# A re-searched instruction order for a fused clustered-attention and gelu kernel, with the last stores on two queues

One core of a Trainium2 chip. The metric is the device time of one execution in microseconds (us), as the median of several executions.

## The reference

Attention over 4 batches x 8 heads (32 "heads" below, numbered 0 to 31), 768 positions, 64 wide, in which a query sees only the keys of its own cluster; then a feed-forward layer without biases.

```python
q_assign = argmax(einsum('bhsd,hcd->bhsc', q_n, c_n), -1)   # 16 clusters; q_n, k_n, c_n normalised
k_assign = argmax(einsum('bhsd,hcd->bhsc', k_n, c_n), -1)
mask   = q_assign[:, :, :, None] == k_assign[:, :, None, :]
scores = where(mask, matmul(q, k^T) / sqrt(D), -1e9)
x      = softmax(scores) @ v          # to 3072 tokens x 512
h      = x @ w_in                     # 512 -> 2048
out    = gelu_exact(h) @ w_out        # 2048 -> 512, float32
```

## The kernel before

Every operation (some matmuls, an exp, a copy, a transfer) is an object with a name, an engine, what it depends on and which buffers it takes. A string, TABLE, lists the names in the order in which they are emitted; `@DVE` behind a name puts that operation on another engine. Nothing is decided at run time: each engine executes its operations in the order of the table, and where an operand isn't there yet, it waits.

```python
TABLE = (
    "cent loadq0 loadq1 zero3 loadk1 dm loadk0 hiq0 zero2 ident ssq ones hik0 exptab root "
    "eps loq0 warm256 warm256 ... warm256 trq0 rnorm lok0 hiq1 loadk2 cn chi warm256 warm256 trk0 "
    # ... cut: about 2000 names ...
    "fc2_3_P7_2_1 u32_3 c222_3@DVE stc2223 fc2_3_P3_2_0 fc2_3_P3_2_1 fc2_3_P4_2_0 "
    "fc2_3_P4_2_1 c122_3 stc1223 c212_3 stc2123 "
)
...
    def run(self, table):
        ...                                        # cut: bookkeeping
        for word in table:
            name, _, eng = word.partition("@")
            if name.startswith("warm"):
                self.filler(int(name[4:]))         # a matmul whose result nobody reads
                continue
            op = by_name[name]
            assert op not in done and done.issuperset(op.deps), name
            ...                                    # cut: takes buffers from their pools
            op.emit(*([eng or op.eng] if op.alt else []))
...
    POOLS = {"raw": 4, "st": 3, "T": 6, ..., "sc": 2, "m": 1, ...}   # buffers of each kind
```

`hi` and `lo` write q and k as a sum of two fp16 numbers into a block `st`; the block is transposed into `kqT`, by TensorE for heads 0 to 9 and by a DMA for heads 10 to 31; then `asn`, the assignment, multiplies it with the centroids.

```python
        if i in PE_TR:                             # heads 0 to 9
            ...                                    # trk / trq on TensorE, evk / evq copy them out
        else:
            def dtr():
                nc.sync.dma_start_transpose(
                    out=new_T().rearrange("p a n d -> p (a n) d"),
                    in_=T["st", i].rearrange("p a n d -> p (a n d)"))
            e = add("SP", 1.4, due - 10, dtr, [sp["k"], sp["q"]], take=[s_T], dma=2.2,
                    name=f"dtr{i}")
            ...
        a1 = add("PE", ad, due + 3, lambda: asn("k"),
                 [ready["k"], c11] + ([ready["q"]] if i > 1 else []), take=[s_m],
                 name=f"asnk{i}")
        a2 = add("PE", ad, due + 3.2, lambda: asn("q"), [ready["q"], a1], name=f"asnq{i}")
```

Names used below: `dtr26` is the DMA transpose of head 26, `asnk26` and `asnq26` its assignment matmuls, `sc` scores (L783 in the kernel before), `av` probabilities times v, `fc1` / `fc2` the two products of the feed-forward layer, `fold`, `amax` and `ge` the steps from the assignment to a one-hot mask, `putk` / `putq` the writing of mask rows into `kqT`, `st...` the stores of results. The middle of each table, which is cut here, is only more of the same.

The softmax here doesn't subtract the row's maximum and nothing guards it: scores larger than these inputs give would overflow.

## Time and profile before

| kernel before | |
|---|---|
| device time, median of 3 (range) | 291.56 us (291.4 to 292.01) |
| span of the core in the profiled run | 289.8 us |
| busy: PE / ACT / DVE / POOL | 98% / 81% / 70% / 37% |
| work of all matmuls, counted by starts | 274.9 us |
| PE idle or stalled inside the span | about 4.6 us of real stalls |

How to read it: the engine names are PE (TensorE), ACT (ScalarE), DVE (VectorE), POOL (GpSimd), SP (SyncE, which issues DMAs). A line of a timeline has the start, the length, the engine, the line of the source, the operation with result<-operands, the size, a count, and in brackets the idle time before it with what ended that. Line numbers of the changed kernels are up to 3 lower than those of the kernel before, since the table is shorter. "By starts" below means: start of a matmul, less the start of the one before, less what the one before needs at full rate (0.109 us for 256 columns, and so on, as the prediction derives). The bracket in a timeline counts from a modelled end and is a little smaller.

### The profile page before, as it was taken

Reading aid. Unit: us, or ns where it says so; the run is one execution under the profiler, and the core shown is the slowest. Engines: PE = TensorE matmul, PEld = TensorE weight load, DVE = VectorE, ACT = ScalarE, POOL = GpSimd, SP = SyncE. Lnnn points to the kernel's source line nnn. Section 1 sums busy time; section 2 is a strip of 40 time slices with the busy share of each in tenths; the row PEclk is TensorE's granted clock in tenths of the full one; section 3 lists DMA queues with packets and bytes.
Section 4 is the critical chain, followed back from the end, with each engine's and each line's share of the span. In section 5 each row is a group of like instructions: output and inputs, shape, how many; then the busy total and the mean of one; then the engine's idle time right before and its main releaser. Section 6 shows DMA issues by size and latency. Waiting matters only on the chain.

```text
span 289.8 us, 8355 instructions
## 1 busy us (share of the span) xinstructions
PE 284.4 (98%) x3398; PEld 213.0 (73%) x3398; DVE 204.2 (70%) x494; ACT 235.1 (81%) x333; POOL 108.0 (37%) x148
## 2 busy tenths in 40 slices
PE   8999999999999999999999999999999999999995
PEld 6887766677677777765677878766687788756884
DVE  4989788397998778643489875725778833787863
ACT  4899988699799999977799988957699988599510
POOL 5898834609120631117202031605622271328000
PEclk9999999999999999999999999999999999999999
DMA  7999998899666799976479899753134213200023
GB/s 249 249 268 248 256 214 230 207 174 177 160 175 139 146 227 187 188 192 168 127 156 177 156 222 187 191 128 75 27 30 118 56 50 97 77 2 0 20 74 127
DMA packets 78038, 43.11 MB, mean 149 GB/s; under 512 B 55472, under 2 KB 78000, under 8 KB 78000
## 3 DMA queue, kind: packets, MB, share of 16 engines
q1 hardware_dynamic: 73488, 38.16, 57.7%
q0 software_dynamic: 4224, 4.19, 8.9%
q8 instruction: 26, 0.43, 0.6%
q10 hardware_dynamic: 288, 0.23, 0.3%
q14 instruction: 12, 0.10, 0.1%
HBM read 27.30 MB, written 6.29 MB: 116 GB/s over the span
## 4 chain that ended last, share of the span: by engine, by line
PE 96%; DVE 2%; ACT 1%; issue 0%; DVEq 0%
PE op L1233 25%; PE hp L918 22%; PE sc_ps L783 21%; PE x_ps L815 12%; PE fx_ps L1054 6%; PE asn_ps L615 2%; PE warm_ps L372 2%; PE tr_ps L573 2%; DVE kqT L714 1%; DVE kqT L723 1%; PE asn_ps L613 1%; PE asn_ps L612 1%; PE oh_ps L691 1%; ACT p_sb L792 1%; PE fin_ps L886 0%
## 5 line engine op out<-in xcount | busy, mean ns | idle before, releaser
L792 ACT ACTIVATE p_sb<-sc_ps 128x768 f16<-128x768 f32 x192 | 146.0, 810 | 9.7 <-PE sc_ps L783 6.8
L783 PE MATMUL sc_ps<-kqT 80*128 80x384 f16 x384 | 93.5, 325 | 0.6 <-DVE kqT L714 0.3
L918 PE MATMUL hp<-xt,w_in_sb 128*128 128x384 f16 x384 | 65.6, 326 | 0.0
L815 PEld LDWEIGHTS <-p_sb 128*128 128x128 f16 x1152 | 47.2, 97 | 10.4 <-DVE x_tok L842 0.6
L1233 PEld LDWEIGHTS <-g 128*128 128x128 f16 x480 | 45.3, 97 | 12.6 <-DVE g L948 0.2
L931 ACT ACTIVATE g<-hp 128x768 f16<-128x768 f32 x48 | 38.9, 810 | 19.0 <-PE hp L918 18.5
L918 PEld LDWEIGHTS <-w_in_sb 128*128 128x128 f16 x384 | 36.4, 98 | 22.9 <-issue 0.2
L815 PE MATMUL x_ps<-vaug,p_sb 128*128 128x65 f16 x1152 | 51.6, 193 | 0.0
L1233 PE MATMUL op<-w_out_sb,g 128*128 128x256 f16 x288 | 40.9, 272 | 0.0
L783 PEld LDWEIGHTS <-kqT 80*128 80x128 f16 x384 | 31.6, 98 | 4.7 <-DVE kqT L714 0.5
L1233 PE MATMUL op<-w_st,g 128*128 128x256 f16 x192 | 27.3, 272 | 0.0
L518 POOL TENSOR_TENSOR st<-k_raw,st 128x384 f16<-128x384 f32 x18 | 17.0, 943 | 24.9 <-DVE st L382 18.4
L518 POOL TENSOR_TENSOR st<-q_raw,st 128x384 f16<-128x384 f32 x21 | 19.8, 947 | 13.4 <-ACT st L380 8.6
L382 POOL CAST st<-q_raw 128x384 f16<-128x384 f32 x16 | 8.4, 531 | 40.9 <-DMA q_raw<-in_q_dram 24.9
L631 DVE TENSOR_REDUCE asb<-asn_ps 128x192 f32<-128x384 f32 x24 | 13.2, 551 | 14.8 <-PE asn_ps L615 14.6
L382 POOL CAST st<-k_raw 128x384 f16<-128x384 f32 x16 | 8.6, 537 | 35.4 <-DMA kqT<-st 16.3
L1233 PEld LDWEIGHTS <-S 128*128 128x128 f16 x192 | 18.0, 97 | 5.0
L842 DVE TENSOR_TENSOR x_tok<-x_ps,rec 128x384 f16<-128x384 f32 (+1 forms) x40 | 19.0, 476 | 1.1
L835 DVE RECIPROCAL rec<-x_ps 128x6 f32<-128x6 f32 (+1 forms) x40 | 7.4, 186 | 11.7 <-PE x_ps L815 10.7
L615 PEld LDWEIGHTS <-kqT 128*128 128x128 f16 x288 | 12.0, 96 | 3.4
L1233 PE MATMUL op<-w_st,S 128*128 128x256 f16 x96 | 13.9, 272 | 0.0
L1233 PE MATMUL op<-w_out_sb,S 128*128 128x256 f16 x96 | 13.8, 272 | 0.0
(125 smaller groups left out, 405.6 us busy)
## 6 DMA issues: line engine op xcount, KB each, us to landing
q_raw<-in_q_dram SPq DMA_DIRECT2D x32, 192.0 KB, 3.5
v_raw<-in_v_dram SPq DMA_DIRECT2D x32, 192.0 KB, 3.5
out_dram<-c SPq DMA_DIRECT2D x48, 128.0 KB, 2.0
k_raw<-in_k_dram SPq DMA_DIRECT2D x31, 192.0 KB, 3.4
w_in_sb<-in_moe_w_in_dram POOLq DMA_DIRECT2D x4, 512.0 KB, 10.4
w_out_sb<-in_moe_w_out_dram POOLq DMA_DIRECT2D x4, 512.0 KB, 8.6
kqT<-st SPq DMA_TRANSPOSE x22, 4.3
k_raw<-in_k_dram ACTq DMA_DIRECT2D x1, 192.0 KB, 3.2
```

Of the source, the lines that this page charges most:

```text
L382: engine[eng].tensor_copy(o, i)
L518: engine[eng].tensor_sub(t[:, :, D:2 * D], T[w + "raw", i], t[:, :, 0:D])
L615: nc.tensor.matmul(o, t[:, js], c_cat[:, h].rearrange("p a c -> p (a c)"), start=True, stop=True)
L631: nc.vector.tensor_reduce(out=T["asb", i], in_=T["asn", i].rearrange("p n w (a c) -> p n w c a", a=2), axis=AX.X, op=ALU.add)
L783: nc.tensor.matmul(s_ps[:, e, 0:QB], T["kT", i][0:D + C, c * 128:(c + 1) * 128], T["qT", i][0:D + C, t * QB:(t + 1) * QB], start=True, sto ...
L792: nc.scalar.activation(T["p", i, t][:, 2 * cp:2 * cp + 2, :], T["sc", i, t, cp][:, :, 0:QB], ACT_FN.Exp, bias=0.0, scale=float(scale))
L815: nc.tensor.matmul(o, T["p", i, t][:, ch, jj * 128:(jj + 1) * 128], vaugs[turn("va", i)][:, ch, 0:D + 1], start=(ch == 0), stop=(ch == N - 1))
L842: nc.vector.tensor_tensor(T["xtok", b][:, h // 2, j0:j0 + nn, h % 2 * D:(h % 2 + 1) * D], T["x", key][:, :, 0:D], T["rec", key].to_broadca ...
L918: nc.tensor.matmul(T["hp", hb, fp][:, e, 0:QB], w_in_sb[:, m, f * 128:(f + 1) * 128], T["xt", b][:, m, t * QB:(t + 1) * QB], start=(m == 0 ...
L931: nc.scalar.activation(T["g", hb][:, :, fp, :], T["hp", hb, fp][:, :, 0:QB], ACT_FN.Gelu, bias=0.0, scale=1.0)
L1054: nc.tensor.matmul(o, a[p](m), r[p](m), start=start and m == 0, stop=m == 1, skip_group_check=not start)
L1233: nc.tensor.matmul(T["op", b, key], a()[:, f, j * 128:(j + 1) * 128], w[:, f, :], start=(start and f == 0), stop=(f == NB - 1), skip_group ...
```

## The change

Its intent: the table had been found by a search against a timing model; it was searched again, with each candidate judged over five samples with noise added to the model, in the hope of an order that holds when durations vary. The new table has the same operations in another order, 145 of them on another engine, and 26 filler matmuls in place of 32. Beside that, the two stores at the end may go to ScalarE's queue.

```diff
-    "cent loadq0 loadq1 zero3 loadk1 dm loadk0 hiq0 zero2 ident ssq ones hik0 exptab root "
-    "eps loq0 warm256 ...                                     (17 more) trq0 rnorm lok0 ..."
+    "ident dm zero2 cent loadq0 ssq ones loadk0 zero3 root eps loadk1 hiq0@POOL rnorm "
+    "hik0 cn lok0 warm256 ...                                 (19 more) trk0 chi clo loq0 ..."
 # ... nearly every line of the table differs; the stretch that matters for head 26:
-    "... exp23b1 dtr26 sc23a0 ... hik30 sc24b1 asnk26 amax27 exp24b1 stc1211 asnq26 fold26 ..."
+    "... exp23a2 loadq31 dtr26 fc2_1_P6_2_1 ... norm22_1 c221_1 asnk26 exp25a1 ... p52_1@ACT asnq26 ..."
 # ... and the end:
-    "... u32_3 c222_3@DVE stc2223 ... c122_3 stc1223 c212_3 stc2123 "
+    "... u32_3 stc2113 c222_3@DVE stc2223@ACT stc1213 ... c212_3 stc2123 stc1223@ACT "
 )
@@ store()
-            st = add("SP", 0.36, due, lambda: nc.sync.dma_start(
+            st = add("SP", 0.36, due, lambda eng: engine[eng].dma_start(
                 out=out_w[b][:, NJ * t + j, col * DB:(col + 1) * DB],
-                in_=T[name, b, j]), [sums_out[name, j]], dma=0.45, name=f"st{name}{j}{b}")
+                in_=T[name, b, j]), [sums_out[name, j]], dma=0.45, name=f"st{name}{j}{b}",
+                alt={"SP": 0.36, "ACT": 0.36} if b == B - 1 and j == 2 else {"SP": 0.36})
```

In the old table `asnk26` stands 70 names behind `dtr26`, in the new one 33.

## The prediction

> **What bounds the kernel now.** I read the page's engine shares first, then the chain that ended last, then the timeline of stretches where the matrix engine could have been waiting.
>
> ```profile
> PE 284.4 (98%) x3398; PEld 213.0 (73%) x3398; DVE 204.2 (70%) x494; ACT 235.1 (81%) x333; POOL 108.0 (37%) x148
> PE 96%; DVE 2%; ACT 1%; issue 0%; DVEq 0%
> ...
> 48.33 7.80 PE hp L918 x48
> 57.08 1.31 PE op L1233 x12
> ```
>
> The engine named PE is busy nearly all the time and carries 96% of the chain (last two lines: time order of that chain; start, length, instruction). But a "busy" matmul overlaps its successor, so I went through the trace matmul by matmul and took starts only: 7.80/48 = 0.162 us for 384 columns, 1.31/12 = 0.109 us for 256, and likewise 0.056 for 128, 0.029 for 65, 0.025 for 32 or 16. Multiplying out all 3398 matmuls gives 274.9 us. The span of 289.8 us is then: 1.36 before the first matmul; 274.9 of work; 2.7 lost in the first 6.8 us, where a filler matmul of 256 columns takes 0.213 (the clock is at half); about 2.9 of irregularities below 15 ns each; 4.6 of real stalls; and 3.4 from where the last matmul has streamed its columns to the end. Only the stalls, the filler matmuls (32 x 0.109 = 3.5 us) and the ends can change: order alone can't touch the 271.4 of useful matmuls.
>
> Where the stalls lie: 2.5 us between 20 and 45 us, 1.6 us later (0.59 of it at 80 to 90), 0.5 before. The 20 to 45 stretch belongs to VectorE (DVE). From the timeline at 19 to 22 us:
>
> ```profile
> 19.63 0.55 DVE L714 TENSOR_SCALAR kqT<-oh_ps 16x768 f16<-16x768 f16 x1 [0.17 <-PE oh_ps L691]
> 20.21 0.55 DVE L723 TENSOR_SCALAR kqT<-oh_ps 16x768 f16<-16x768 f16 x1
> 20.79 0.56 DVE L714 TENSOR_SCALAR kqT<-oh_ps 16x768 f16<-16x768 f16 x1
> 21.39 0.56 DVE L723 TENSOR_SCALAR kqT<-oh_ps 16x768 f16<-16x768 f16 x1
> ...
> 22.00 0.50 PE L783 MATMUL sc_ps<-kqT 80*128 80x384 f16 x2 [0.20 <-DVE kqT L723]
> ```
>
> Four mask rows written one behind the other; the score of head 3 starts when the fourth ends, 0.36 us after PE was free by its starts. So until the first feed-forward block (44.6 us) PE and DVE are about equally loaded, and a gain needs both.
>
> A second kind of stall comes where ScalarE changes from gelu back to exp. Timeline at 54 to 59 us:
>
> ```profile
> 56.17 0.81 ACT L931 ACTIVATE g<-hp 128x768 f16<-128x768 f32 x1 [0.49 <-PE hp L918]
> ...
> 57.00 1.28 ACT L792 ACT_TABLE_LOAD   x1
> 58.23 0.49 PE L783 MATMUL sc_ps<-kqT 80*128 80x384 f16 x2
> 58.29 2.21 ACT L792 ACTIVATE p_sb<-sc_ps 128x768 f16<-128x768 f32 x3
> ...
> 59.15 0.48 PE L783 MATMUL sc_ps<-kqT 80*128 80x384 f16 x2
> ```
>
> Two PSUM buffers serve scores and hidden products. After the last hidden product (its first matmul starts at 54.69) come its gelu, the table load and one exp; only then is a buffer free for the third score, at 59.15. That is 4.46 us, for which the order before has 4.30 us of other PE work: a stall of 0.16.
>
> **The Trainium skill.** "TensorE: Matmul & The Clock Gate", Back-to-back issue gap, gives columns/2.4 + 2.5 ns at full clock: 162.5, 109 and 56 ns for 384, 256 and 128 columns, and the trace agrees to a nanosecond. The same page, What's actually happening, has the array start at half clock and go full after about 3.4 us of activity, at a point that varies. Here the full rate comes 5.4 us after the first matmul; the loss is an amount of time, so it should be the same in both kernels. "SBUF — State Buffer", SBUF: two separate sides, says that a VectorE instruction in a two-port mode, or with two SBUF inputs, and a GpSimd instruction lock each other out. The cast of the centroids agrees: 0.82 us at 5.67 us, while GpSimd's subtraction ran from 5.47 to 6.41. "DMA: Bandwidth & Descriptors", Issuing engines are not separate DMA queues: issuing from two engines saves only the sequencer's issue time. I use that for the tail.
>
> **The change, part by part.** The set of operations is the same; the table has 6 filler matmuls fewer (32 to 26), 145 operations have another engine, and nearly every position moves. Two stores of the last row tile go to ScalarE's queue.
>
> 1. Filler: 6 x 0.109 = 0.65 us less PE work. All of it lies before head 3. It counts only if the real work can start earlier.
>
> 2. Start. Before, k0's rest is done on DVE at 5.48 and q0's earlier; q0's and k0's transposes stood behind 18 and 2 fillers. After, 20 fillers (1.36 + 20 x 0.213 = 5.6) lead to k0's transpose, whose input should again be ready at 5.5. So there is nothing to gain there; q0's cast is now on GpSimd behind the square root (3.5 to 4.07 before, so about 4.6), and its rest on DVE comes after the centroids' cast and difference (about 6.0 to 6.7). q0's transpose then starts at 6.6 to 7.3, its evacuation ends at 7.9 to 8.6 (8.08 before), and one DVE subtraction (0.55) precedes the first maximum as before. The first score moves by -0.4 to +0.3 us, middle -0.1.
>
> 3. Up to the first feed-forward block. From the first evacuation on, the durations of the trace add up to 34.0 us of DVE work through the last evacuation of the first batch before, and 33.4 after (a subtraction, one transposed block and one evacuation leave DVE for GpSimd or ScalarE; two casts come in). Up to the masks of head 3 the sums are equal (13.9 and 13.9), so that stall stays, and grows by what PE arrives earlier: much of the 0.65 is absorbed there. DVE's 0.6 less should show as the block starting earlier: -0.6 with -0.1 from the start and about +0.2 for waits I can't see. The first block starts 0.5 us earlier. By then PE has 237.5 us of work left in place of 237.9: another -0.33.
>
> 4. Changes from gelu to exp. PE work between the last hidden product and the third score, before: 4.30, 4.25, 4.36, 4.45; after: 4.42, 4.42, 4.51, 4.47. Against the 4.46 needed the stalls are 0.16, 0.21, 0.10, 0.01 before (the trace has 0.16, 0.19, 0.08, 0) and 0.04, 0.04, 0, 0 after: -0.35. The fourth score after the second change waited 0.14 and has 0.17 us more room: -0.14. Together -0.5. The opposite changes, exp to gelu, need about 3.4 and have 3.9 or more in both. The number of table loads is 10 in both.
>
> 5. Tail. The timeline of the end:
>
> ```profile
> 285.57 1.04 PE L1233 MATMUL op<-w_st,g 128*128 128x256 f16 x8
> 285.77 0.42 DVE L1285 TENSOR_TENSOR c<-u,op 128x256 f32<-128x256 f32 x1
> 286.65 0.42 DVE L1279 TENSOR_TENSOR c<-p,op 128x256 f32<-128x256 f32 x1 [0.45 <-PE op L1233]
> ```
>
> The last result is ready at 287.07 and its store is issued at 287.10; the store before it left SyncE at 286.67. So the queue was free for 0.43 us, and a second queue removes no wait. The order of the last matmuls and results is the same. I give it 0.
>
> Sum: -0.5 - 0.33 - 0.5 - 0 = -1.3 us of 291.56, that is 290.3.
>
> **The rivals.** (a) Start and DVE win nothing: GpSimd gets 19 us more work (110 to 129 by the trace's durations), mostly subtractions with two inputs, so more DVE instructions meet its lock. Some 24 DVE instructions were stretched before, by up to 1 us. For it: in the first 40 us of PE work GpSimd's share rises from 33 to 41 us, and it also makes the operands of the transposes. Against it: DVE's own sum falls by some 5 us, and elsewhere a stretched instruction mostly isn't waited for. It would leave 291.0 to 291.6, in a bad case 292. (b) The order search finds nearly all the stalls: 4.6 down to 2, with the whole 0.65 kept. For it: five noisy samples favour orders with room, and the changes of table show just that. Against it: the stalls where two PSUM buffers and a string of exps limit (sums of shortfall 0.69 before, 0.67 after, at 1.33 us from one score to the next but one) are as tight as they were. It would make 288.3 to 289. (c) The tail gains: if the other queue's completion overlaps better, up to 0.4 us; the free queue speaks against it.
>
> **Range and chances.** My terms are uncertain by about 0.4 for the start, 0.5 for the first batch and 0.4 for stalls I can't foresee later; together about 0.8 us. The range is 289.2 to 291.4. Faster by 2% means below 285.7; with no stall left and six fillers fewer it would still be 291.56 - 4.6 - 0.65 = 286.3, so 0.02. Slower by 2% means 297.4, which would take a new wait of 6 us; with all orders kept dependency-safe, 0.01. Within 2%: 0.97.
>
> **What would show it.** Right: starts of matmuls add up to 274.2; the first hidden product starts at 44.1 (44.6 before); no PE stall over 0.06 us at the third score behind a gelu-to-exp load; last result to end still 2.7 us. Wrong: a first score later than 11.5 us (11.15 before); DVE waits or stretched DVE instructions on the chain between 12 and 44 us; new stalls between 90 and 250 us, where the kernel before has only some 0.6; or a shorter tail.

## The result, and the profile after

| | before | after |
|---|---|---|
| median (range, runs) | 291.59 us (291.4 to 292.01, 4) | 291.57 us (291.08 to 291.66, 4) |
| ratio after / before, 95% interval | | 0.9994 (0.9977 to 1.0011) |
| span of the profiled run | 289.8 us | 289.3 us |

A ratio here is the mean time of one kernel's fast runs over that of the other's of the same rounds, so not quite the ratio of the medians. The time is the same; 290.3 was predicted and 291.57 lies just above the range. The profiled run of the changed kernel happened to be its fastest, 291.08.

The page of the changed kernel, its shares and its chain by engine:

```profile
PE 282.8 (98%) x3392; PEld 211.9 (73%) x3392; DVE 203.8 (70%) x487; ACT 230.7 (80%) x323; POOL 129.3 (45%) x165
...
PE 88%; DMA 6%; DVE 2%; POOL 1%; ACT 1%; issue 0%; ACTq 0%; SPq 0%; POOLq 0%
```

GpSimd has the predicted 129 us. The chain, which was 96% PE and had no DMA in it, now runs for 6% through DMAs. A chain walks back from the end; that it leaves PE for DMAs says that somewhere PE was released by one. What PE waited for, first before, then after (line, released by: us in total, times, longest):

```profile
PE warm_ps L372 <- DVE dm L401: 1.4, 1, 1.4
PE sc_ps L783 <- DVE kqT L714: 0.3, 1, 0.3
PE tr_ps L573 <- DVE kqT L714: 0.2, 1, 0.2
PE sc_ps L783 <- DVE kqT L723: 0.2, 1, 0.2
```

```profile
PE warm_ps L371 <- DVE dm L400: 1.4, 1, 1.4
PE asn_ps L614 <- DMA kqT<-st: 1.0, 2, 0.8
PE chl_ps L449 <- DVE cent_hl L441: 0.5, 1, 0.5
PE tr_ps L572 <- DVE st L517: 0.2, 1, 0.2
```

The first line of both is the time before the first matmul. The two waits for mask rows (`sc_ps <- DVE kqT`) are gone. In their place stand two waits of an assignment for a DMA-transposed block, 1.0 us, and two at the start. Where they are, from the changed kernel's timeline; first head 18, then head 26:

```profile
114.61 0.49 PE L782 MATMUL sc_ps<-kqT 80*128 80x384 f16 x2
115.34 0.47 PE L614 MATMUL asn_ps<-c_cat,kqT 128*128 128x32 f16 x12 [0.23 <-DMA kqT<-st]
...
173.82 1.69 SPq L588 DMA_TRANSPOSE kqT<-st  x1
...
177.98 0.60 PE L1233 MATMUL op<-w_st,g 128*128 128x256 f16 x4
...
179.34 0.32 PE L614 MATMUL asn_ps<-c_cat,kqT 128*128 128x32 f16 x6 [0.75 <-DMA kqT<-st]
```

By starts PE stood 115.34 - 114.61 - 2 x 0.162 = 0.40 us before head 18 and 179.34 - 177.98 - 4 x 0.109 = 0.92 us before head 26. The transpose of head 26 was issued at 173.82 and its block had landed 5.5 us later. The kernel before issued that transpose at nearly the same time, but came to the assignment six microseconds later:

```profile
174.10 1.88 SPq L589 DMA_TRANSPOSE kqT<-st  x1
...
185.24 0.46 PE L615 MATMUL asn_ps<-c_cat,kqT 128*128 128x32 f16 x12
```

There 11.1 us lie between issue and use, and no wait is shown. For head 18 the distance was 10.1 us. In the changed kernel the two distances are 5.5 and 5.4 us, but the waits are in them: without its wait PE would have come to head 26's block 4.6 us after the issue and to head 18's 5.0 us after. The page's median from issue to landing of such a transpose is 4.3 us before and 4.5 after, so both look just safe until one looks at the transfer concerned: head 26's block took 6.0 us to land in the profile of the kernel before (4.0 in that of e6, which has the same order there), and the prediction did not look at it. Nor is a short distance enough to tell: head 16's block had 4.7 us in the changed kernel and made no wait, since it landed in 3.7.

The same story without brackets: the start of chosen matmuls in the profiled runs (us from the start of the span). The last two columns are two experiments told below, the changed kernel run again and a mended order.

| matmul | before | after | after, again (e1) | mended (e4) |
|---|---|---|---|---|
| first score | 11.15 | 11.08 | 11.19 | 11.40 |
| first feed-forward block | 44.60 | 43.69 | 43.79 | 44.01 |
| first score after the second batch of gelu | 144.16 | 142.67 | 143.27 | 142.42 |
| first hidden product of the third batch | 187.50 | 186.87 | 187.87 | 185.80 |
| end of the matmuls | 286.45 | 285.92 | 286.92 | 284.87 |
| span | 289.8 | 289.3 | 290.3 | 288.4 |

Up to the third row the changed kernel is 1.49 us ahead, which is more than was predicted in all (0.89 when run again). Between the third and the fourth row it takes 44.20 us (44.60 when run again) where the kernel before takes 43.34: 0.86 to 1.26 us of the lead goes there, and head 26 lies in it. After the fourth row the two take the same (98.95 and 99.05).

### The profile page after: what moved, and what is told of

Same layout as the page of the kernel before. It is cut to its first block, busy times and chain, and to the rows that moved or that the text cites. A ratio compares the mean times of both kernels' runs of the same rounds, so it can differ in the third digit from the quotient of the medians.

```text
span 289.3 us, 8351 instructions
## 1 busy us (share of the span) xinstructions
PE 282.8 (98%) x3392; PEld 211.9 (73%) x3392; DVE 203.8 (70%) x487; ACT 230.7 (80%) x323; POOL 129.3 (45%) x165
## 4 chain that ended last, share of the span: by engine, by line
PE 88%; DMA 6%; DVE 2%; POOL 1%; ACT 1%; issue 0%; ACTq 0%; SPq 0%; POOLq 0%
PE op L1233 23%; PE hp L917 22%; PE sc_ps L782 19%; PE x_ps L814 10%; PE fx_ps L1053 6%; DMA kqT<-st 4%; PE asn_ps L614 2%; PE tr_ps L572 2%; DMA q_raw<-in_q_dram 1%; DMA k_raw<-in_k_dram 1%; PE asn_ps L611 1%; PE asn_ps L612 1%; PE oh_ps L690 1%; PE fin_ps L885 1%; POOL st L517 1%
## 5 line engine op out<-in xcount | busy, mean ns | idle before, releaser
L814 PEld LDWEIGHTS <-p_sb 128*128 128x128 f16 x1152 | 48.3, 97 | 10.9 <-DVE x_tok L841 0.9
L814 PE MATMUL x_ps<-vaug,p_sb 128*128 128x65 f16 x1152 | 52.6, 193 | 0.0
L1233 PE MATMUL op<-w_out_sb,g 128*128 128x256 f16 x288 | 40.3, 272 | 0.1
L517 POOL TENSOR_TENSOR st<-k_raw,st 128x384 f16<-128x384 f32 x26 | 24.8, 957 | 21.8 <-DVE st L381 18.3
L517 POOL TENSOR_TENSOR st<-q_raw,st 128x384 f16<-128x384 f32 x19 | 18.2, 965 | 7.5 <-DVE st L381 7.1
L381 POOL CAST vaug<-v_raw 128x384 f16<-128x384 f32 x21 | 11.1, 529 | 20.5 <-DMA v_raw<-in_v_dram 13.4
L1293 POOL TENSOR_TENSOR c<-u,p 128x256 f32<-128x256 f32 x6 | 4.5, 754 | 26.8 <-ACT p L379 13.1
L381 POOL CAST st<-k_raw 128x384 f16<-128x384 f32 x13 | 6.9, 532 | 21.2 <-DMA k_raw<-in_k_dram 18.1
L614 PEld LDWEIGHTS <-kqT 128*128 128x128 f16 x288 | 11.4, 96 | 4.3 <-DMA kqT<-st 1.7
L713 DVE TENSOR_SCALAR kqT<-ohT 16x768 f16<-16x768 f16 x23 | 13.2, 575 | 0.7 <-DMA ohT<-oh 0.3
```

Of the source, the lines that this page charges most:

```text
L381: engine[eng].tensor_copy(o, i)
L517: engine[eng].tensor_sub(t[:, :, D:2 * D], T[w + "raw", i], t[:, :, 0:D])
L614: nc.tensor.matmul(o, t[:, js], c_cat[:, h].rearrange("p a c -> p (a c)"), start=True, stop=True)
L814: nc.tensor.matmul(o, T["p", i, t][:, ch, jj * 128:(jj + 1) * 128], vaugs[turn("va", i)][:, ch, 0:D + 1], start=(ch == 0), stop=(ch == N - 1))
L1233: nc.tensor.matmul(T["op", b, key], a()[:, f, j * 128:(j + 1) * 128], w[:, f, :], start=(start and f == 0), stop=(f == NB - 1), skip_group ...
```

## The experiments

Twelve runs of 5 or 6 executions each, in four jobs; the kernels of a job and runs of the kernel before were timed on the same chip. The theory: the new order is as good as predicted except where an assignment follows its DMA transpose too closely. Rivals: GpSimd's extra work stretches VectorE and that costs the time; the second queue costs something; the removed fillers or the new start cost something; or there was no gain to lose.

| run | edit | median us (range, runs) | ratio to before (95%) |
|---|---|---|---|
| e1 | the changed kernel again | 291.94 (291.34 to 293.06, 6) | 1.0011 (0.999 to 1.0033) |
| e2 | its stores on one queue | 293.06 (291.63 to 294.11, 6) | 1.0052 (1.0029 to 1.0076) |
| e3 | head 26's assignment later | 290.44 (290.05 to 291.63, 6) | 0.996 (0.994 to 0.9981) |
| e4 | e3, and head 18's transpose sooner | 290.13 (289.84 to 290.55, 6) | 0.9946 (0.9929 to 0.9963) |
| e5 | e4, one queue | 290.71 (290.57 to 291.15) | 0.9964 (0.9951 to 0.9977) |
| e6 | before, six fillers fewer | 291.66 (291.27 to 292.08) | 0.9993 (0.998 to 1.0007) |
| e7 | e4, three more places | 290.56 (289.83 to 290.82) | 0.9955 (0.9939 to 0.9971) |
| e8 | after, head 26's transpose sooner | 290.94 (290.68 to 291.32) | 0.9972 (0.9958 to 0.9985) |
| e9 | e4, one queue in the old order | 290.58 (289.9 to 292.12) | 0.9967 (0.9947 to 0.9987) |
| e10 | e4, a cast sooner and a mask row on DVE | 290.43 (289.83 to 290.92, 5) | 0.9955 (0.9942 to 0.9968) |
| e11 | e4 again | 290.49 (289.84 to 291.31) | 0.9968 (0.9956 to 0.998) |
| e12 | e4, the cast sooner alone | 290.58 (290.42 to 291.02, 6) | 0.996 (0.9948 to 0.9972) |

The kernel before had medians of 291.73, 291.64, 291.57 and 291.74 in the four jobs (11 runs each): e1 to e4 are of the first, e5 to e8 of the second, e9 to e11 of the third, e12 of the fourth. All results were correct.

**e1_again.** No edit.

> The changed kernel once more, unaltered, for its spread and a second profile. Its four runs so far were 291.08, 291.66, 291.61 and 291.53, and the profile is of the 291.08 one. If the waits for transposed blocks (0.92 us before the assignment of head 26, 0.40 before that of head 18) are fixed features of the order, a second profile shows them again within 0.2 us each and the median is 291.3 to 291.7. If they are chance, another profile has them elsewhere.

Measured: the same as before, as in the first comparison, though 0.2 us over the expected median. The profiled run (292.07) had the two waits again, 0.53 us before head 18 and 1.22 before head 26 (0.1 and 0.3 more than the first time). The view names another releaser for the second:

```profile
178.68 0.60 PE L1231 MATMUL op<-w_st,g 128*128 128x256 f16 x4
...
180.34 0.32 PE L612 MATMUL asn_ps<-c_cat,kqT 128*128 128x32 f16 x6 [1.06 <-DVE amax L643]
```

A maximum on VectorE ended within 0.01 us of that start, and the inference took it. But nothing in the assignment reads that maximum; the PSUM buffer that it needs had been free for 1.75 us, and the last piece of head 26's block landed 0.05 us before the start. So it is the transpose, 5.6 us after its issue.

**e2_one_queue.** The second part of the change undone.

```diff
-    stc2113 c222_3@DVE stc2223@ACT stc1213 ... c212_3 stc2123 stc1223@ACT
+    stc2113 c222_3@DVE stc2223     stc1213 ... c212_3 stc2123 stc1223
```

> The changed kernel with all stores on SyncE. My step 5 says the second queue is worth 0: time equal to the changed kernel within 0.1 us, last result to end 2.7 to 2.8 us in both. The rival, that the second queue costs something at the end (another queue to be drained) or gains by overlap, would show 0.2 us or more between the two in that distance and in the time.

Measured: 1.1 us slower than e1 by the medians. The profiled run, the fastest, shows 0.5 of it: from the last matmul's columns to the end 3.88 us in place of 3.39, because in this order `stc1223`, whose result is ready first, now stands behind `stc2123`, and is issued 1.03 us after the last matmul (with two queues it went out 0.10 before that, and the last store of all at 0.65). Runs up to 294.11 aren't explained by it. So in the new order the second queue matters; whether it is worth anything against the old order took e9.

**e3_asn26_later.** One word moved: the assignment of k of head 26 goes to just before that of q, 29 names later.

```diff
-    norm22_1 c221_1 asnk26 exp25a1 c211_1 u22_1 sc25a0 ... sc24a2 p52_1@ACT        asnq26
+    norm22_1 c221_1        exp25a1 c211_1 u22_1 sc25a0 ... sc24a2 p52_1@ACT asnk26 asnq26
```

> The changed kernel, with the first half of head 26's assignment moved 30 places later, next to its second half; nothing depends on it earlier. Theory (new waits for DMA-transposed blocks ate the gain): the 0.92 us wait goes, at most 0.2 comes back elsewhere, time 0.7 to 0.9 us below the changed kernel's, about 290.7. Rival (the stall is slack that another limit, ScalarE's exps or VectorE, would impose a few us later): the lost time at the next change of stage stays within 0.3 us of before, and the time stays at 291.3 or more.

Measured: 0.4% faster than the kernel before, 1.5 us by the medians faster than e1, more than the 0.7 to 0.9 expected. This is the largest effect of any single edit, and it touches neither an engine's load nor the number of operations. The wait before head 18 was still there (0.31 us).

**e4_two_transposes.** And the transpose of head 18 one place sooner in SyncE's queue.

```diff
-    putq16 av14b0 av14b1 dtr21 dtr18 av14a1
+    putq16 av14b0 av14b1 dtr18 dtr21 av14a1
```

> As the run before, and the transposes of heads 18 and 21 swapped on SyncE, so that 18's, which is needed first, is issued some 1.7 us earlier (head 21 is needed 10.9 us after its issue). Theory: the 0.40 us wait before head 18's assignment goes too, time 1.1 to 1.3 us below the changed kernel's, about 290.3. Rival: no better than the run before.

Measured: 290.13, the lowest median of all, and the narrowest range of the first job. First what PE waited for in all, then from the timeline the place of head 26's old wait:

```profile
PE warm_ps L369 <- DVE dm L398: 1.4, 1, 1.4
PE tr_ps L570 <- DVE st L515: 0.9, 2, 0.7
PE chl_ps L447 <- DVE cent_hl L439: 0.5, 1, 0.5
```

```profile
177.74 0.60 PE L1231 MATMUL op<-w_st,g 128*128 128x256 f16 x4
...
178.29 0.48 PE L780 MATMUL sc_ps<-kqT 80*128 80x384 f16 x2
178.61 0.89 PE L812 MATMUL x_ps<-vaug,p_sb 128*128 128x65 f16 x24
```

No DMA in the list any more, and the score follows the product 0.55 us later, 0.11 over its 0.436, in place of 1.36. In the table of starts above, the stretch between the third and fourth row is back to 43.38 us (43.34 before), and the rest takes 99.07 as ever. So the lead was real and the two waits ate it: e3 and e4 change nothing else. What the second edit alone is worth, the times do not show: its wait is gone from the profile, but e11, this same kernel in another job, had 290.49 against e3's 290.44. (The 0.9 us in the list is at the start, on a profile that also came late to its first score, 11.40; e11's has 0.2 there and 11.10.)

**e5_e4_one_queue.** e4 with the stores on SyncE, and `stc1223` put ahead of the last result.

```diff
-    u32_3 stc2113 c222_3@DVE stc2223@ACT stc1213 ... fc2_3_P4_2_1         c212_3 stc2123 stc1223@ACT
+    u32_3 stc2113 c222_3@DVE stc2223     stc1213 ... fc2_3_P4_2_1 stc1223 c212_3 stc2123
```

> The run with both transposes mended (290.13 us), with all stores on SyncE and the last two in the order of the kernel before (the one that is ready first goes first). The earlier one-queue run kept the order of the two-queue table, so the store that was ready first stood behind the other, and last result to end grew by 0.5 us. Theory (the second queue is worth 0 by itself): time within 0.15 us of 290.1, last matmul to end 3.4 us as before. Rival (the second queue gains by itself): 290.5 or more, last matmul to end 3.7 or more.

Measured: 290.71, and 4.12 us from the last matmul to the end. Four stores stand one behind the other on SyncE from 284.50 on; the last of them is issued some 0.7 us after the last result is ready (285.35). `stc1213`, ready long before, stood behind `stc2223`, whose result came late. So this was no fair undo: in a queue, one late result holds up all that come after it. e9 puts that right.

**e6_before_six_fewer.** The kernel before, with 6 of the 7 fillers behind the centroids' transpose taken out.

```diff
-    ctr evq0@DVE hik1 lok1@DVE cc warm256 warm256 warm256 warm256 warm256 warm256 warm256 asnk0
+    ctr evq0@DVE hik1 lok1@DVE cc warm256 asnk0
```

> The kernel before, with six of the seven fillers behind the centroids' transposes left out. My step 1 counts 0.65 us less PE work. What the changed kernel's trace shows (0.68 and 0.32 us of waiting for VectorE before the first assignment in place of the fillers) says the work there is bounded by VectorE and the fillers only fill: first score and time unchanged within 0.15 us. Rival (fillers delay the real work): 0.3 to 0.65 us less.

Measured: 0.9993, nothing. The first score starts at 11.38 us, against 11.15 with the fillers: a wait took their place. The prediction's 0.65 us of removed fillers were worth nothing by themselves.

**e7_more_order.** e4 with three further places changed at which its profile showed a stall.

```diff
-    stc1110 fc1_1_5_1 putq11@ACT gelu1_0
+    stc1110 fc1_1_5_1 putq11     gelu1_0
-    stc1200 ge14 fc2_0_P5_1_0 amax15 loadv17 ... hiq16 sc13a1              fc2_0_P5_1_1
+    stc1200 ge14              amax15 loadv17 ... hiq16 sc13a1 fc2_0_P5_1_0 fc2_0_P5_1_1
-    exp27a2 S4_23 sc28a1 ge30 rec26_1 ... norm26_1 fc2_2_P7_0_0        exp28a1
+    exp27a2 S4_23        ge30 rec26_1 ... norm26_1 fc2_2_P7_0_0 sc28a1 exp28a1
```

> The run with both transposes mended, and three more moves at stalls that all its profiles share: head 28's score behind the next feed-forward product (0.27 us), a feed-forward product behind the next score (0.18), one mask row from ScalarE to VectorE among gelus (0.16). If each stall is local, 0.4 to 0.6 us less than 290.13, about 289.6. If other limits (two PSUM buffers, ScalarE) take their place, 290.0 to 290.3.

Measured: no gain over e4. The stalls aimed at are gone from the profile; new ones of 0.54 and 0.37 us at 91 to 93 us and of 0.43 at 225 came.

**e8_dtr26_earlier.** The other way to mend head 26: leave the assignment, and issue the transpose two places sooner on SyncE.

```diff
-    sc22a0       ohd24 hik28@DVE av21a2 ... exp23a2 loadq31 dtr26 fc2_1_P6_2_1
+    sc22a0 dtr26 ohd24 hik28@DVE av21a2 ... exp23a2 loadq31       fc2_1_P6_2_1
```

> The changed kernel, with the transpose of head 26 issued one place earlier on SyncE, ahead of the mask transpose of head 24 (issue at about 171.9 in place of 173.8), the matrix engine's order untouched. If the place in SyncE's queue made the wait, the 0.9 to 1.2 us before head 26's assignment fall to 0.2 or less, and time to about 290.7, unless head 24's masks now come late (then as much is lost at its first score). If the transfers share of the DMA engines or the completion itself is what lags, landing does not move and the wait stays over 0.6 us.

Measured: 290.94, in between. First the place of the old wait in this run, then one line of the changed kernel beside it (PEld is TensorE's weight load; here the block is the weight):

```profile
172.01 1.41 SPq L586 DMA_TRANSPOSE kqT<-st  x1
...
173.52 1.58 SPq L692 DMA_TRANSPOSE ohT<-oh  x1
...
177.92 0.60 PE L1231 MATMUL op<-w_st,g 128*128 128x256 f16 x4
...
178.17 0.56 DVE L628 TENSOR_REDUCE asb<-asn_ps 128x192 f32<-128x384 f32 x1
178.25 0.10 PEld L612 LDWEIGHTS <-kqT 128*128 128x128 f16 x1
...
178.78 0.30 PE L612 MATMUL asn_ps<-c_cat,kqT 128*128 128x32 f16 x6 [0.26 <-DVE asb L628]
```

```profile
179.34 0.22 PEld L614 LDWEIGHTS <-kqT 128*128 128x128 f16 x6 [1.03 <-DMA kqT<-st]
```

Issued 1.8 us sooner, the block landed 3.5 us sooner: at 175.78, 3.76 us after the issue, where the changed kernel's took 5.47 and those of the ten other profiles with this transpose in its old place 5.5 to 6.2. The weight load that reads it starts at 178.25, right behind the product, and no longer waits for a DMA. A wait of 178.78 - 177.92 - 0.436 = 0.42 us is left, but for something else: there is one PSUM buffer for assignments (`"m": 1` in POOLS), and VectorE empties it of head 27's only at 178.73 (178.17 + 0.56). In the changed kernel VectorE started that at 177.34. It came late here because the transpose of head 24's one-hot mask now stands behind head 26's block, is issued at 173.52 in place of 171.88, and VectorE's four mask rows run from 176.67 on in place of 174.99. So the place in SyncE's queue did make head 26's wait, and taking it from another transfer made a smaller one, as the expectation had named for head 24's masks. Moving the reader (e3) left no wait there.

**e9_one_queue_old_order.** e4 with one queue, and both stores of early results ahead of those of late ones, as in the table before.

```diff
-    u32_3 stc2113 c222_3@DVE stc2223@ACT stc1213 ... fc2_3_P4_2_1 c212_3 stc2123 stc1223@ACT
+    u32_3 stc1213 stc2113 c222_3@DVE stc2223 ... fc2_3_P4_2_1 stc1223 c212_3 stc2123
```

> All stores on SyncE, and now all three stores that the two-queue table had put late stand where the kernel before has them (the earlier one-queue run had one of them stuck behind a store whose result came 3 us later: last matmul to end 4.1 us, 0.6 more). Theory (the second queue only frees the order of the stores; with the old order it is worth 0): time and last matmul to end within 0.15 us of the two-queue kernel beside it. Rival (two queues gain by themselves): 0.3 us or more slower, last matmul to end 3.7 or more.

Measured: 290.58 against e11's 290.49 of the same job. From the last matmul to the end 3.66 us against 3.46. By itself the second queue is worth nothing that these runs could tell from zero: 0.09 us by the medians, 0.2 by the tails of the profiles, where e9's interval alone is 0.6 us to either side.

**e10_cast_and_mask.** e4 with two edits at the waits that were left: a cast at the start sooner on ScalarE, a mask row back to VectorE.

```diff
-    ctr evk0      hik1 cc loadk2 hiq1 trq0
+    ctr evk0 hiq1 hik1 cc loadk2      trq0
-    stc1110 fc1_1_5_1 putq11@ACT gelu1_0
+    stc1110 fc1_1_5_1 putq11     gelu1_0
```

> The kernel with both transposes mended, and two moves. At the start ScalarE casts q1 ahead of k1, so GpSimd's subtraction for k1 starts later and should no longer lock out VectorE's difference of the centroids (0.82 us there, 0.23 where it runs free). One mask row of head 11 goes from ScalarE to VectorE among gelus. If the lock bounds the start, the difference takes 0.2 to 0.3, the wait between the two centroid transposes falls from 0.5 to 0.7 to under 0.2, the first score comes 0.3 to 0.5 us earlier, and the time falls by 0.3 to 0.6 with the 0.16 at the mask row. If the start is bounded by loads or by what follows on VectorE, the first score moves by less than 0.15 and only the 0.16 is won.

Measured: no gain over e11 that the runs could tell, but a clear view of the lock between VectorE and GpSimd. The start, first of the changed kernel, then of e10:

```profile
5.49 0.97 POOL L517 TENSOR_TENSOR st<-k_raw,st 128x384 f16<-128x384 f32 x1 [0.62 <-ACT st L379]
...
5.73 0.82 DVE L441 TENSOR_TENSOR cent_hl<-cent_n,cent_hl 128x64 f16<-128x64 f32 x1
...
6.69 0.22 PE L449 MATMUL chl_ps<-ident,cent_hl 128*128 128x128 f16 x1 [0.51 <-DVE cent_hl L441]
```

```profile
5.78 0.23 DVE L439 TENSOR_TENSOR cent_hl<-cent_n,cent_hl 128x64 f16<-128x64 f32 x1
...
6.01 0.36 PE L447 MATMUL chl_ps<-ident,cent_hl 128*128 128x128 f16 x2
...
7.14 0.92 POOL L515 TENSOR_TENSOR st<-k_raw,st 128x384 f16<-128x384 f32 x1 [2.21 <-ACT st L377]
```

In the changed kernel GpSimd's subtraction starts just before the centroids' small difference on VectorE, which then takes 0.82 us in place of 0.23; the second centroid transpose waits for it. With the casts swapped, GpSimd's input comes 1.6 us later and both transposes run together. The first score starts 0.37 us sooner (10.73, against 11.10 in e11), as expected, but the third only 0.19 (12.34 against 12.53): a transpose between them now waits 0.25 us for one of GpSimd's subtractions.

**e11_two_transposes_again.** No edit against e4.

> The kernel with both transposes mended once more, as the reference for the two runs beside it on this chip. 289.9 to 290.5, no wait over 0.15 us before the assignments of heads 18 and 26.

Measured: 290.49, 0.3% below the kernel before. With e4, twelve runs of 289.84 to 291.31, all but the slowest below the fastest run of the kernel before in these jobs (291.07).

**e12_with_cast.** e10's cast alone.

> The kernel with both transposes mended and q1 cast ahead of k1 at the start, without the mask row's move (that move brought a new wait of 0.53 us at 91 us in both runs that had it). If the waits are local: 0.2 us less than the mended kernel, some 1.3 us less than the kernel before, about 290.2, the first score at 12.3 to 12.4 in the profile (12.5 to 12.8 without), no wait over 0.2 us at 91 us. Rival: the mask row's move was not the cause of the wait at 91 us, and it is here again.

Measured: the stall at 91 us that e7 and e10 have isn't there, so the mask row's move made it, as far as one profile can tell. The first score is at 10.92, but the third at 12.53, no sooner than in e11 (the 12.3 to 12.8 of the expectation are the third score's). This profile has a new wait of 0.51 us before head 24's assignment, for its DMA transpose, at a place where e1 showed 0.08: these landings vary from run to run.

## Why the prediction was wrong

**The failed step is the one that put later stalls at zero, with "0.4 for stalls I can't foresee later" as its uncertainty.** The prediction looked at what could get better, and named new stalls between 90 and 250 us as what would make it wrong, but it never compared the distance from each DMA transpose to its reader in the two tables. The stalls over 0.06 us in that stretch add up to 0.45 us before, 1.82 in the changed kernel, and 0.64 in e4. The assignment of head 26 had moved six microseconds towards a transpose that is issued when it was before. That and head 18 cost 1.3 us in the profiled run and 1.75 in e1's, about the whole of the predicted -1.3. Taking those two waits away, and nothing else, gave 290.13 and 290.49 where 290.3 had been predicted for the changed kernel. The other terms were about right: in e4's profile the span is 1.44 us shorter than before, of which 0.59 come before the first feed-forward block (0.5 predicted), 0.99 after it (0.33 + 0.5), and the tail takes 0.14 back (0).

**Step 1, fillers, and step 2, start.** The matmul work is 274.2 us, as counted. The first score moved by -0.07 us, within the step's -0.4 to +0.3. Taking out fillers was worth 0 (e6), since waits take their place: 3.26 us are lost by PE in the first 8 us, against 2.65 before. That the loss at half clock would be the same in both kernels was wrong: the full rate came 5.4 us after the first matmul before, 4.0 in the changed kernel and 3.2 in e4's profile, but waits filled what that freed. Step 3's -0.33 is another thing: matmuls that the new order does before the first block and not after it.

**Step 3, first batch.** Predicted -0.5 at the first feed-forward block; -0.91 in the profiled run, -0.6 to -1.0 in the ten profiles that have this start. The stalls between 11.7 and 44 us went from 2.71 to 1.61 us, which the prediction had held for unlikely: it expected head 3's stall to grow.

**Step 4, gelu to exp.** Right. The third scores waited 0.04, 0, 0 and 0 us, against 0.16, 0.19, 0.08 and 0, and the fourth score's 0.14 is gone.

**Step 5, tail.** Right: 3.39 us from the last matmul's columns to the end, 3.37 before. The end of the changed kernel's timeline:

```profile
285.34 0.84 ACTq L1212 DMA_DIRECT2D out_dram<-c  x2
...
286.12 0.42 DVE L1279 TENSOR_TENSOR c<-p,op 128x256 f32<-128x256 f32 x1 [0.34 <-PE op L1233]
286.57 0.33 SPq L1212 DMA_DIRECT2D out_dram<-c  x1
```

The last result ends at 286.54 and its store is issued at 286.57, from a queue that had nothing else to do, just as before. e9 confirms it.

**Rival (a), GpSimd.** Its lock is real: VectorE instructions more than 0.09 us over their usual length went from 23 (10.8 us over, in all) to some 34 (16 us over), and VectorE's busy time fell from 204.2 to 203.8 us only, where the prediction saw some 5 us less. But e4 has as many (38, 16 us over) and is faster, so this is not what cost the gain. On the path are only the 0.59 us at the start, where removing it gained nothing that the runs could tell (e10, e12), and a mask row at 59 us, which made PE stall by 0.22. Its number, 291.0 to 291.6, came true for another reason. **Rival (c)**, a gain at the tail, didn't come. **Rival (b)**, 288.3 to 289, was reached by no order that was run; the best had 290.13.

**What stays open.** Why the changed kernel's runs spread (291.1 to 293.1 in all, e4's first six within 0.7 us): landings that vary are consistent with it (0.92 to 1.22 us before head 26, 0.19 to 0.53 before head 18 in three profiles), but only profiled runs show them, and e1's profile also lost some 0.3 us at 71 us. Why e2 had runs of 294: the slowest, 294.11, had a granted clock of 0.994 (as had e9's slowest, 292.12), but the next, 293.57, had 1.0.

## What to carry to other kernels

When an order changes, list for every transfer the distance from issue to first reader in both orders, and hold each against the landing time of that very transfer in the traces you have, not against a median; where the trace shows a wait, take it off the distance first. A saving early in a kernel that is bound by one engine is kept only as far as no later wait, for something that runs on its own clock, stands in the way: follow the lead from landmark to landmark, and the place where it shrinks names the culprit. Then look first whether the reader can move: here that cost nothing, while issuing the transfer sooner delayed another one behind it, and through it a buffer.

## What the Trainium skill lacked or had wrong

- "Advanced Engine Details and Errata", X-Bar Transpose (TRN2), says that such transposes are as fast as regular DMAs. No run here has a regular DMA of the same size beside them: the 393 KB transposes between SBUF tiles (a size worked out from the kernel) had a median of 4.3 us from issue to landing before and 4.5 after, the 192 KB loads 3.4 to 3.5 and 3.8 to 4.2; the transposes that made PE wait for 0.1 us or more took 4.8 to 5.6. No page gives a time from issue to landing for a transpose in a queue with others under way.
- "DMA: Bandwidth & Descriptors", Issuing engines are not separate DMA queues: agrees as far as the runs can tell: one queue against two made 0.1 us (e9, e11) when the order of the stores was right. That section has nothing on a late result's store holding up ready ones behind it in one queue, which cost some 0.5 us of tail in e2 and 0.6 in e5.
- "SBUF — State Buffer", SBUF: two separate sides: agrees, with 0.82 us in place of 0.23 for the small difference beside a GpSimd subtraction.
- "TensorE: Matmul & The Clock Gate", Back-to-back issue gap, gives some 81 ns for each matmul of 128 columns in a stream in which each has its own weight load. The transposes here, six of 128 columns with six weight loads, follow each other at 56 ns.
- "TensorE: Matmul & The Clock Gate", What's actually happening: agrees that the moment of full rate varies, but gives ±500 ns. From the first matmul it took 5.4 us in the profile before, 4.0 in the changed one, and 2.7 (e2) and 3.2 (e4) in others.
